# Feed-forward first layers by seven block products in place of eight, and phases that alternate

## Chip, cores and metric

The kernel runs on one core of a Trainium2 chip. The metric is the device time of one execution in microseconds (us).

## What is computed

Attention with a mask by clusters, then two feed-forward networks, all in float32. The attention is not touched by the change; what follows it is:

```python
x = attention(q, k, v, centroids)               # 1536 tokens x 512
p = domain_probs / (domain_probs.sum(-1, keepdims=True) + 1e-9)
y = 0
for e in range(4):                              # first network: w1[e] 512x1024, w2[e] 1024x512
    h = maximum(x @ w1[e], 0)
    y += p[:, e:e+1] * (h @ w2[e])
h = y @ w_in                                    # second network: 512x2048
out = maximum(0.01 * h, h) @ w_out              # 2048x512
```

## The kernel before, in words

The hidden columns of both networks are cut into 24 chunks of 256 (`FCH`): 16 of the first network (`c < N1`, four per expert) and 8 of the second. A chunk has a first layer, h, for three blocks of 512 tokens (`u`), and a second, y, for 12 output tiles of 128 x 512 that add up in `acc`. Float32 accuracy comes from splitting each operand in a high and a low part (hi, lo, of type float32r) and adding three matmuls, hi·hi, hi·lo and lo·hi. So the first layer of a chunk is 3 token blocks x 2 column blocks of 128 x 4 blocks of the 512 model dimensions x 3 = 72 matmuls (`h_products`, L622), and the second is 12 tiles x 2 x 3 = 72 (`emit_y1`, L772 to L774; in the second network `emit_y2`, L790 to L792). All of these have 512 columns.

Behind a block of h (`h_finish`): VectorE forms g from the PSUM result (L634; in the second network ScalarE scales first, L638, and VectorE takes the maximum, L639), ScalarE writes its high part (L119) and GpSimd its low part (L120). Behind a tile of y VectorE adds it to `acc` (L779, L797). The weights of a chunk come by DMA, are split by ScalarE and GpSimd, and in the second network (where the inputs hold 64-bit numbers) are first narrowed by one ScalarE and four VectorE instructions per matrix (L180 to L190).

The order of the work is the order in which the code emits it. The loop at the end runs over the chunks, and the first layer of chunk c+1 is emitted between the tiles of the second layer of chunk c: a block h(c+1, u), then four tiles of y(c), and so on:

```python
for i in range(NTILE):
    if i % KC == 0:
        emit_h(c + 1, i // KC)
    (emit_y1 if c < N1 else emit_y2)(c, i)
```

For this the split weights `w1s`, `w2s` and the split hidden values `hbuf` exist twice, and chunk c uses set c % 2. Set 0 of `w1s` and `hbuf` is made in a pool `early` at the right end of SBUF (it is filled while the attention still runs), set 1 and both sets of `w2s` in the pool `ffn`. In the built program the tiles of `early` start 32 bytes past a multiple of 64 (`w1hi0` at 182240, `hhi0` at 194528), those of `ffn` at multiples of 128. At the step from the first network to the second (chunk 15) the result y is split again as the new x, tile by tile, by ScalarE and GpSimd, and h(16, 0) is emitted ahead of the last four tiles. In PSUM h has two buffers of two banks, y four of one bank.

## Time and profile before

| | us |
|---|---|
| runs | 1059.11, 1059.86, 1064.7; median 1059.86 |
| the profiled execution | 1058.93 |
| its span | 1057.1 |
| TensorE busy in it | 1028.7 (97%), 6182 matmuls |
| VectorE, ScalarE, GpSimd busy | 558.6, 358.9, 457.9 |

The span runs from the first to the last instruction of the profiled execution; its time has 1.83 us around it. Matmuls overlap in the pipeline, so a matmul's own duration (0.39 us) is longer than the distance to the next; distances are read between starts.

### The profile page before, as it was taken

What the parts mean: (1) busy time and instruction counts of PE and PEld (TensorE: products, weight loads), DVE (VectorE), ACT (ScalarE), POOL (GpSimd) and SP (SyncE); (2) the same over time, 40 slices, a digit from 0 to 9 for tenths busy, and PEclk for the clock granted to TensorE, in tenths of its full rate; (3) what the DMA queues carried; (4) which work ended last, traced back from release to release, by engine and by line L of the source; (5) the groups of instructions that cost most, each with busy time, mean ns of one, the idle gap of its engine ahead of it and who ended that gap; (6) DMA issues with size and microseconds to landing.
All of it is one profiled execution on the core that took longest, in us unless ns stands there. A gap on an engine that the chain in (4) does not pass through costs nothing.

```text
span 1057.1 us, 14668 instructions
## 1 busy us (share of the span) xinstructions
PE 1028.7 (97%) x6182; PEld 843.4 (80%) x6184; DVE 558.6 (53%) x744; ACT 358.9 (34%) x435; POOL 457.9 (43%) x232
## 2 busy tenths in 40 slices
PE   7799999999999999999999999999999999999998
PEld 4678888887888888888888888888877888888886
DVE  7698888886113333334333343333572376555754
ACT  3577777784320111101111011110243432323320
POOL 4367777771632433324333343323475333333331
PEclk8899999999999999999999999999999999999999
DMA  7855666440301112111111111110210212212003
GB/s 187 171 119 114 135 136 135 105 104 13 115 15 40 40 40 54 17 40 41 40 46 25 40 40 40 35 46 20 80 42 38 80 51 69 77 43 80 4 37 120
DMA packets 59530, 70.71 MB, mean 67 GB/s; under 512 B 25060, under 2 KB 42088, under 8 KB 59464
## 3 DMA queue, kind: packets, MB, share of 16 engines
q1 hardware_dynamic: 59464, 69.77, 25.2%
q8 instruction: 49, 0.80, 0.3%
q14 instruction: 17, 0.14, 0.0%
HBM read 46.19 MB, written 3.17 MB: 47 GB/s over the span
## 4 chain that ended last, share of the span: by engine, by line
PE 84%; DVE 9%; SPq 2%; POOL 2%; ACT 2%; DMA 1%; issue 1%; DVEq 0%; ACTq 0%
PE big L622 37%; PE y L774 8%; PE y L773 8%; PE y L772 8%; PE y L791 4%; PE y L790 4%; PE y L792 4%; DVE m L401 3%; PE big L397 2%; PE big L432 2%; PE big L433 1%; PE small L458 1%; PE small L460 1%; PE small L459 1%; PE big L266 1%
## 5 line engine op out<-in xcount | busy, mean ns | idle before, releaser
L120 POOL TENSOR_TENSOR hlo<-g,hhi 128x1024 fp32r<-128x1024 f32 x72 | 176.3, 2449 | 446.7 <-ACT hhi L119 446.7
L622 PE MATMUL big<-xlo,w1hi 128*128 128x512 f32 x576 | 226.8, 394 | 1.0 <-POOL xlo L120 1.0
L622 PE MATMUL big<-xhi,w1hi 128*128 128x512 f32 x576 | 226.8, 394 | 0.5 <-DVE xlo L120 0.5
L622 PE MATMUL big<-xhi,w1lo 128*128 128x512 f32 x576 | 226.1, 392 | 0.0
L119 ACT ACTIVATE hhi<-g 128x1024 fp32r<-128x1024 f32 x72 | 76.3, 1060 | 437.2 <-DVE g L634 406.2
L634 DVE SCALAR_TENSOR_TENSOR g<-big,pb 128x1024 f32<-128x1024 f32 x48 | 58.8, 1225 | 241.8 <-PE big L622 234.4
L446 POOL TENSOR_TENSOR plo<-p,phi 128x768 f16<-128x768 f32 x84 | 138.1, 1655 | 82.2 <-ACT phi L445 46.4
L779 DVE TENSOR_TENSOR acc<-y,acc 128x512 f32<-128x512 f32 x180 | 124.1, 691 | 90.5 <-PE y L774 87.7
L774 PE MATMUL y<-hlo,w2hi 128*128 128x512 f32 x384 | 151.2, 394 | 0.0
L772 PE MATMUL y<-hhi,w2hi 128*128 128x512 f32 x384 | 150.7, 392 | 0.5 <-DVE acc L779 0.5
L773 PE MATMUL y<-hhi,w2lo 128*128 128x512 f32 x384 | 150.8, 393 | 0.0
L622 PEld LDWEIGHTS big<-xlo,w1hi 128*128 128x128 f32 x576 | 108.3, 188 | 26.4 <-POOL xlo L120 2.2
L622 PEld LDWEIGHTS big<-xhi,w1hi 128*128 128x128 f32 x576 | 108.2, 188 | 25.6 <-DVE xlo L120 0.9
L622 PEld LDWEIGHTS big<-xhi,w1lo 128*128 128x128 f32 x576 | 108.3, 188 | 24.6
L401 DVE TENSOR_REDUCE m<-big 128x1 f32<-128x768 f32 x96 | 90.3, 949 | 14.1 <-PE big L397 12.9
L435 ACT ACTIVATE p<-big 128x768 f32<-128x768 f32 x96 | 77.6, 809 | 34.7 <-PE big L433 32.8
L772 PEld LDWEIGHTS y<-hhi,w2hi 128*128 128x128 f32 x384 | 72.2, 188 | 17.4 <-DVE acc L779 0.9
L773 PEld LDWEIGHTS y<-hhi,w2lo 128*128 128x128 f32 x384 | 72.1, 188 | 16.6
L774 PEld LDWEIGHTS y<-hlo,w2hi 128*128 128x128 f32 x384 | 72.1, 188 | 16.3
L639 DVE TENSOR_TENSOR g<-big,g 128x1024 f32<-128x1024 f32 x24 | 29.4, 1225 | 88.0 <-ACT g L638 88.0
L791 PE MATMUL y<-w2lo,hhi 128*128 128x512 f32 x192 | 75.5, 393 | 0.0
L790 PE MATMUL y<-w2hi,hhi 128*128 128x512 f32 x192 | 75.4, 393 | 0.0
(134 smaller groups left out, 1577.7 us busy)
## 6 DMA issues: line engine op xcount, KB each, us to landing
qkb<-pair SPq DMA_DIRECT2D x32, 384.0 KB, 6.8
w1raw<-in_moe_w_dram SPq DMA_DIRECT2D x16, 512.0 KB, 3.4
w2raw<-in_moe_w_dram SPq DMA_DIRECT2D x16, 512.0 KB, 3.6
w1raw<-in_moe_w_in_dram SPq DMA_DIRECT2D x8, 1024.0 KB, 5.3
w2raw<-in_moe_w_out_dram SPq DMA_DIRECT2D x8, 1024.0 KB, 4.8
qka<-pair SPq DMA_DIRECT2D x16, 384.0 KB, 4.0
vraw<-in_v_dram SPq DMA_DIRECT2D x16, 192.0 KB, 2.9
pb<-pe_rows SPq DMA_DIRECT2D x4, 768.0 KB, 8.1
```

The lines of the kernel that those rows point to most:

```text
L119: nc.scalar.activation(out=hi, in_=src, func=AF.Copy)
L120: lo_engine.tensor_tensor(out=lo, in0=src, in1=hi.bitcast(F32), op=ALU.subtract)
L401: nc.vector.tensor_reduce(out=m_t[t][:, j:j + 1], in_=ps[:, 0:S], op=ALU.max, axis=AX.X)
L435: nc.scalar.activation(out=p_t[t, kb], in_=ps[:, 0:S], func=AF.Exp, scale=scale)
L446: (nc.vector if plo_on_vector else nc.gpsimd).tensor_tensor(out=plo, in0=p, in1=phi, op=ALU.subtract)
L622: nc.tensor.matmul(pv[:, f, :], lhsT=w[:, kc, fs], rhs=x[:, kc, us], start=kc + i == 0, stop=kc == KC - 1 and i == 2,)
L772: nc.tensor.matmul(ps, lhsT=whi[:, f, ks], rhs=hi[:, f, us], start=f == 0, stop=False)
L773: nc.tensor.matmul(ps, lhsT=wlo[:, f, ks], rhs=hi[:, f, us], start=False, stop=False)
L774: nc.tensor.matmul(ps, lhsT=whi[:, f, ks], rhs=lo[:, f, us], start=False, stop=f == NF - 1)
L779: nc.vector.tensor_tensor(out=a, in0=ps, in1=a, op=ALU.add)
L790: nc.tensor.matmul(ps, lhsT=hi[:, f, ts], rhs=whi[:, f, :], start=f == 0, stop=False)
L791: nc.tensor.matmul(ps, lhsT=hi[:, f, ts], rhs=wlo[:, f, :], start=False, stop=False)
```

## The change

- In the four chunks 0, 1, 16 and 17 (`PLAIN`) the first layer stays at 72 matmuls. In the other 20 (`emit_seven`) token block 0 stays plain (24 matmuls), and blocks 1 and 2 are one 2 x 2 x 2 block product (two column blocks of 128, two halves of 256 model dimensions, two token blocks) by the Strassen-Winograd scheme: seven products of six matmuls each (`product`) in place of eight, 42 in place of 48.
- The scheme needs sums. Of the weights: s1 to s4, four GpSimd instructions of 128 x 256 per chunk and a split of the result (`weights_sums`). Of x: t1 to t4, once per network, by VectorE, ScalarE and one GpSimd instruction (`input_sums`). Of the products: five additions on VectorE (`plus`) and one copy on ScalarE per chunk, through three SBUF tiles `part`; products that belong to one sum are added up in PSUM.
- Instead of h(c+1) between the tiles of y(c), the whole first layer of a chunk runs, then its whole second layer, then the next chunk. There is one set of `w1s`, `w2s` and `hbuf`, which is set 0; the sums s and t lie in `ffn`. PSUM is eight tiles of one bank: 0 to 5 for h, four in turn (6, 7, 2, 3) for y.
- g, hi and lo of h are made per column block, 128 x 512 in place of 128 x 1024; low parts of weights in two halves. The narrowed weights go straight to the raw tiles. The first `acc` copies (chunks 0 and 16) go from ScalarE to VectorE, and a third of the low parts of the new x from GpSimd to VectorE.

What the order of instructions shows, at the three places that matter. First VectorE, in a chunk of the first network: y, big and z are PSUM tiles, pb the probabilities. Before:

```order
L634 SCALAR_TENSOR_TENSOR g0_3478<-big0_5156,pb1_4216 128x1024
L779 TENSOR_TENSOR acc_4218<-y1_5184,acc_4218 128x512
L779 TENSOR_TENSOR acc_4218<-y2_5192,acc_4218 128x512
L779 TENSOR_TENSOR acc_4218<-y3_5200,acc_4218 128x512
L779 TENSOR_TENSOR acc_4218<-y0_5208,acc_4218 128x512
L634 SCALAR_TENSOR_TENSOR g0_3478<-big1_5216,pb1_4216 128x1024
```

Now, from the second column block of token block 0 to the second tile of y:

```order
L656 SCALAR_TENSOR_TENSOR g1_4208<-z1_6074,pb0_3476 128x512
L895 TENSOR_TENSOR part_4218<-z3_6117,part_4218 128x512
L895 TENSOR_TENSOR part_4218<-z4_6131,part_4218 128x512
L656 SCALAR_TENSOR_TENSOR g0_3475<-z2_6075,pb0_3476 128x512
L895 TENSOR_TENSOR part_4218<-z5_6142,part_4218 128x512
L895 TENSOR_TENSOR z4_6131<-z4_6131,part_4218 128x512
L656 SCALAR_TENSOR_TENSOR g0_3475<-part_4218,pb0_3476 128x512
L656 SCALAR_TENSOR_TENSOR g1_4208<-z4_6131,pb0_3476 128x512
L895 TENSOR_TENSOR z5_6142<-z5_6142,part_4218 128x512
L656 SCALAR_TENSOR_TENSOR g1_4208<-z5_6142,pb0_3476 128x512
L944 TENSOR_TENSOR acc_4210<-z7_6173,acc_4210 128x512
L944 TENSOR_TENSOR acc_4210<-z2_6184,acc_4210 128x512
```

The five additions and four of the six g stand together ahead of the first tile of y. TensorE waits for the second and third of these additions before it adds further products into z4 and z5.

Then GpSimd, in a chunk of the first network. Before:

```order
L120 TENSOR_TENSOR hlo1_4214<-g0_3478,hhi1_4213 128x2x512
L120 TENSOR_TENSOR w1lo0_3474<-w1raw_3475,w1hi0_3473 128x1024
L120 TENSOR_TENSOR w2lo1_4212<-w2raw_4217,w2hi1_4211 128x1024
L120 TENSOR_TENSOR hlo1_4214<-g1_4215,hhi1_4213 128x2x512
```

Now:

```order
L192 TENSOR_TENSOR w1lo0_3471<-w1raw_3472,w1hi0_3470 128x512 x2
L204 TENSOR_TENSOR sums_4213<-w1raw_3472 128x256
L205 TENSOR_TENSOR sums_4213<-sums_4213,w1raw_3472 128x256
L206 TENSOR_TENSOR sums_4213<-w1raw_3472 128x256
L207 TENSOR_TENSOR sums_4213<-w1raw_3472,sums_4213 128x256
L192 TENSOR_TENSOR slo_4215<-sums_4213,shi_4214 128x512 x2
L120 TENSOR_TENSOR hlo0_3474<-g1_4208,hhi0_3473 128x512 x2
L192 TENSOR_TENSOR w2lo0_4206<-w2raw_4207,w2hi0_4205 128x512 x2
L120 TENSOR_TENSOR hlo0_3474<-g0_3475,hhi0_3473 128x512 x2
L120 TENSOR_TENSOR hlo0_3474<-g1_4208,hhi0_3473 128x512 x2
```

Five instructions per chunk have become sixteen smaller ones; the split of the weights for the next chunk and their sums now follow the last low parts of h.

And TensorE at a step from the first layer to the second. Before (chunk c in y, chunk c+1 in h):

```order
L774 MATMUL y0_5148<-hlo0_3477,w2hi0_4209 128x512
L622 MATMUL big0_5156<-xhi_66,w1hi1_4207 128x512
L622 MATMUL big0_5156<-xlo_67,w1hi1_4207 128x512
L622 MATMUL big0_5156<-xhi_66,w1lo1_4208 128x512
...
L772 MATMUL y1_5184<-hhi0_3476,w2hi0_4209 128x512
```

Now (the last product of a chunk, and its own y):

```order
L862 MATMUL z5_6142<-xhi_63,shi_4214 128x512
L862 MATMUL z5_6142<-xlo_64,shi_4214 128x512
L862 MATMUL z5_6142<-xhi_63,slo_4215 128x512
...
L937 MATMUL z7_6173<-hhi0_3473,w2hi0_4205 128x512
```

The y that follows reads the h that was just made, from the same set 0. Over the whole program TensorE has 120 rows less (7644 in place of 7764).

The diff, cut to its core:

```diff
-    psum = ctx.enter_context(tc.tile_pool(name="psum", bufs=1, space=bass.MemoryType.PSUM))
 
     st_main = ExitStack()
     st_prep = ExitStack()
     psum_a = st_main.enter_context(tc.tile_pool(name="psum_a", bufs=1, space=bass.MemoryType.PSUM))
-    bigs = [(psum, "big0"), (psum, "big1"), (psum_a, "big2")]
+    bigs = [(psum_a, "big0"), (psum_a, "big1"), (psum_a, "big2")]
     smalls = [(psum_a, "small0"), (psum_a, "small1")]
-    turns = [0, 0]
+    turns = [0, 0, 0]
...
-    def weights_split(c, part):
-
-        if c >= NCH:
-            return []
-        hi, lo = (w1s, w2s)[part][c % 2]
-        if not (wide and chunks[c][3] is None):
-            return [lambda: split(hi, lo, raw12[part], nc.gpsimd)]
+    def weights_narrow(c, part):
 
         w = raw64[part].rearrange("p k (f t) -> p k f t", t=2)
         low, high = w[:, :, :, 0], w[:, :, :, 1]
-        f = ffn.tile(list(hi.shape), F32, tag="narrow", name="narrow", bufs=2)
+        f = raw12[part]
...
-            lambda: split(hi, lo, f, nc.gpsimd),
+        ]
+
+    def split_halves(hi, lo, src):
+
+        nc.scalar.activation(out=hi, in_=src, func=AF.Copy)
+        n = src.shape[1] // 2
+        for x in (slice(0, n), slice(n, 2 * n)):
+            nc.gpsimd.tensor_tensor(out=lo[:, x], in0=src[:, x], in1=hi.bitcast(F32)[:, x], op=ALU.subtract)
+
+    def weights_split(part):
+        hi, lo = (w1s, w2s)[part][0]
+        split_halves(hi, lo, raw12[part])
+
+    def weights_sums():
+
+        r = raw12[0]
+        a11, a12, a21, a22 = [r[:, 2 * k:2 * k + 2, 128 * f:128 * f + 128] for f in range(2) for k in range(2)]
+        s1, s2, s3, s4 = [sums[:, n] for n in range(4)]
+        return [
+            lambda: nc.gpsimd.tensor_tensor(out=s1, in0=a21, in1=a22, op=ALU.add),
+            lambda: nc.gpsimd.tensor_tensor(out=s2, in0=s1, in1=a11, op=ALU.subtract),
+            lambda: nc.gpsimd.tensor_tensor(out=s3, in0=a11, in1=a21, op=ALU.subtract),
+            lambda: nc.gpsimd.tensor_tensor(out=s4, in0=a12, in1=s2, op=ALU.subtract),
+            lambda: split_halves(shi, slo, sums),
         ]
...
-        whi, wlo = w1s[c % 2]
+        whi, wlo = w1s[0]
...
-    def h_finish(c, u):
-        hi, lo = [x[:, :, u * 512:(u + 1) * 512] for x in hbuf[c % 2]]
-        pv = h_ps.pop((c, u)).rearrange("p (f t) -> p f t", f=NF)
-        g = gbuf[u % len(gbuf)]
+    def h_split(c, u, f, src, between=None):
+
+        nf = src.shape[1]
+        hi, lo = [x[:, f:f + nf, u * 512:(u + 1) * 512] for x in hbuf[0]]
+        if nf == NF:
+            g = gbuf[turns[2] // 2 % 2]
+        else:
+            g = gbuf[turns[2] // 2 % 2][:, turns[2] % 2:turns[2] % 2 + 1, :]
+        turns[2] += nf
         if c < N1:
+            if between:
+                between()
             p = pbuf[chunks[c][3] % 2][:, :, u * 512:(u + 1) * 512]
             nc.vector.scalar_tensor_tensor(
-                out=g, in0=pv, scalar=0.0, in1=p.to_broadcast([128, NF, 512]), op0=ALU.max, op1=ALU.mult,
+                out=g, in0=src, scalar=0.0, in1=p.to_broadcast([128, nf, 512]), op0=ALU.max, op1=ALU.mult,
             )
         else:
-            nc.scalar.activation(out=g, in_=pv, func=AF.Copy, scale=0.01)
-            nc.vector.tensor_tensor(out=g, in0=pv, in1=g, op=ALU.max)
+            nc.scalar.activation(out=g, in_=src, func=AF.Copy, scale=0.01)
+            if between:
+                between()
+            nc.vector.tensor_tensor(out=g, in0=src, in1=g, op=ALU.max)
         split(hi, lo, g, nc.gpsimd)
 
+    def h_finish(c, u):
+        h_split(c, u, 0, h_ps.pop((c, u)).rearrange("p (f t) -> p f t", f=NF))
...
-    bigs.pop()
-    smalls[:] = [(psum_f, f"y{n}") for n in range(4)]
-    w1_set(ffn)
     w2_set(ffn)
-    w2_set(ffn)
-    h_set(ffn)
     raw12.append(ffn.tile([128, FCH // 128, DM], F32, name="w2raw"))
+    gbuf.append(ffn.tile([128, FCH // 128, 512], F32, name="g1"))
+    pbuf.append(ffn.tile([128, 1, NT], F32, name="pb1"))
     acc = ffn.tile([128, NTILE * DM], F32, name="acc")
     acc_t = acc.rearrange("p (k t) -> p k t", k=KC)
     acc_n = acc.rearrange("p (i d) -> p i d", i=NTILE)
-    if wide:
-        raw64 = [
-            ffn.tile([128, KC, 2 * FCH], I32, name="w1raw64"), ffn.tile([128, FCH // 128, 2 * DM], I32, name="w2raw64"),
+    raw64 = [
+        ffn.tile([128, KC, 2 * FCH], I32, name="w1raw64"), ffn.tile([128, FCH // 128, 2 * DM], I32, name="w2raw64"),
+    ]
+
+    sums = ffn.tile([128, 4, 2, 128], F32, name="sums")
+    shi, slo = [ffn.tile([128, 4, 2, 128], F32R, name=f"s{x}") for x in ("hi", "lo")]
+    thi, tlo = [ffn.tile([128, 4, 2, 512], F32R, name=f"t{x}") for x in ("hi", "lo")]
+    part = ffn.tile([128, 3, 1, 512], F32, name="part")
+
+    BANKS = ((0, 1), (2, 3), (4, 5))
+
+    def bank(n):
+        return psum_f.tile([128, 1, 512], F32, tag=f"z{n}", name=f"z{n}")
+
+    def y_bank():
+        turns[1] += 1
+        return bank((6, 7, 2, 3)[turns[1] % 4])[:, 0, :]
...
+    def product(ps, w, x, first):
+
+        for k in range(2):
+            for i, j in ((0, 0), (0, 1), (1, 0)):
+                nc.tensor.matmul(
+                    ps[:, 0, :], lhsT=w[i][:, k, :], rhs=x[j][:, k, :], start=first and k + i + j == 0,
+                    stop=k == 1 and i == 1, skip_group_check=True,
+                )
+
...
+    def emit_seven(c, steps):
+
+        w = w1s[0]
+        a11, a12, a21, a22 = [
+            [x[:, 2 * k:2 * k + 2, 128 * f:128 * f + 128] for x in w] for f in range(2) for k in range(2)
         ]
+        s1, s2, s3, s4 = [[x[:, n] for x in (shi, slo)] for n in range(4)]
+        t1, t2, t3, t4 = [[x[:, n] for x in (thi, tlo)] for n in range(4)]
+        x11, x21, x22 = [
+            [x[:, 2 * k:2 * k + 2, 512 * u:512 * u + 512] for x in (xhi, xlo)] for k, u in ((0, 1), (1, 1), (1, 2))
+        ]
+        copy, u2, u3 = part[:, 0], part[:, 1], part[:, 2]
+
+        def some(n):
+            for _ in range(n):
+                if steps:
+                    steps.pop(0)()
+
+        def plus(out, ps, other):
+            nc.vector.tensor_tensor(out=out, in0=ps, in1=other, op=ALU.add)
+
+        p0, p1, pa = bank(0), bank(1), bank(2)
+        after = [] if c + 1 < NCH and is_wide(c + 1) else steps[:]
+        steps = [] if after else steps
+        some(3)
+        plain(c, 0, 0, p0)
+        product(pa, a11, x11, True)
+        h_split(c, 0, 0, p0, lambda: nc.scalar.activation(out=copy, in_=pa, func=AF.Copy))
+        some(2)
+        plain(c, 0, 1, p1)
+        h_split(c, 0, 1, p1)
+        weights_split(1)
+        steps += after
+        some(len(steps))
+        pb = bank(3)
+        product(pb, s2, t2, True)
+        plus(u2, pb, copy)
+        product(pa, a12, x21, False)
+        pc = bank(4)
+        product(pc, s3, t3, True)
+        plus(u3, pc, u2)
+        h_split(c, 1, 0, pa)
+        pd = bank(5)
+        product(pd, s1, t1, True)
+        plus(u3, pd, u3)
+        product(pc, a22, t4, False)
+        plus(pc, pc, u2)
+        h_split(c, 2, 1, u3)
+        h_split(c, 1, 1, pc)
+        product(pd, s4, x22, False)
+        plus(pd, pd, u2)
+        h_split(c, 2, 0, pd)
...
-        ps = small()
+        ps = y_bank()
...
-            nc.scalar.activation(out=a, in_=ps, func=AF.Copy)
+            nc.vector.tensor_copy(out=a, in_=ps)
...
-            split(xhi[:, k, us], xlo[:, k, us], a, nc.gpsimd)
+            split(xhi[:, k, us], xlo[:, k, us], a, nc.gpsimd if u < 2 else nc.vector)
...
-    for u in range(1, NU):
-        emit_h(0, u)
+    turns[1] = 0
+    PLAIN = (0, 1, N1, N1 + 1)
+    sums_left, quota = [], []
     for c in range(NCH):
-        turn = c == N1 - 1
-        steps = weights_split(c + 2, 0) + [lambda: weights_load(c + 3, 0)]
-        steps += weights_split(c + 1, 1) + [lambda: weights_load(c + 2, 1)]
+
+        steps = []
+        if c + 1 < NCH and is_wide(c + 1):
+            steps += weights_narrow(c + 1, 0)
+            if c + 2 < NCH:
+                steps.append(lambda: weights_load(c + 2, 0))
+        if c + 1 < NCH and not is_wide(c + 1):
+            steps.append(lambda: weights_load(c + 1, 1))
+        if c in PLAIN:
+            weights_split(1)
+            if c == 0:
+                sums_left = input_sums(False)
+                quota = [5, 5, 5, 5]
+            n = quota.pop(0)
+            slots = steps + sums_left[:n]
+            sums_left = sums_left[n:]
+            blocks = [(u, f) for u in range(1 if c == 0 else 0, NU) for f in range(NF)]
+            for n, (u, f) in enumerate(blocks):
+                if c > 0:
+                    ps = bank(BANKS[u][f])
+                    plain(c, u, f, ps)
+                elif f == 0:
+                    both_ps = [bank(BANKS[u][f]) for f in range(NF)]
+                    for k in range(KC):
+                        for g in range(NF):
+                            plain(c, u, g, both_ps[g], [k])
+                if c == 0:
+                    ps = both_ps[f]
+                h_split(c, u, f, ps)
+                for _ in range(-(-len(slots) // (len(blocks) - n))):
+                    step = slots.pop(0)
+                    if step:
+                        step()
+        else:
+            emit_seven(c, steps)
...
+            steps.append(lambda: weights_split(0))
+            if c + 1 not in PLAIN:
+                steps += weights_sums()
...
-        steps.reverse()
+        steps = [x for pair in zip_longest(steps, later) for x in pair if x]
         for i in range(NTILE):
-            if i % KC == 0:
-                u = i // KC
-                if turn and u == NU - 1:
-                    emit_h(c + 1, 0)
-                elif not turn and c + 1 < NCH:
-                    emit_h(c + 1, u)
+            if c == N1 - 1 and i == NTILE - 1:
+                sums_left = input_sums(True)
+                quota = [3, 2, 4, 4]
+                sums_left.pop(0)()
             (emit_y1 if c < N1 else emit_y2)(c, i)
-            for _ in range(2 if len(steps) > NTILE - 1 - i else 1):
-                if steps:
-                    steps.pop()()
-        if turn:
-            for u in range(1, NU):
-                emit_h(c + 1, u)
+            for _ in range(-(-len(steps) // (NTILE - i))):
+                steps.pop(0)()
 
 
 # ---- launch: one core; inputs and outputs as the reference has them ----
```

## Rows read from the trace of the kernel before

**Rows 1.** The page, part 1, the whole span.

```profile
span 1057.1 us, 14668 instructions
PE 1028.7 (97%) x6182; PEld 843.4 (80%) x6184; DVE 558.6 (53%) x744; ACT 358.9 (34%) x435; POOL 457.9 (43%) x232
```

**Rows 2.** TensorE, who waited for whom, 250 us to end: us, times, longest.

```profile
PE big L622 <- POOL xlo L120: 1.0, 2, 0.8
PE big L622 <- DVE xlo L120: 0.5, 1, 0.5
PE y L772 <- DVE acc L779: 0.5, 1, 0.5
```

**Rows 3.** Order of time, TensorE: start, us, line, operation; first matmul of a block.

```profile
258.84 0.50 PE L622 MATMUL big<-xhi,w1hi 128*128 128x512 f32 x1 [0.49 <-DVE xlo L120]
...
469.61 0.39 PE L622 MATMUL big<-xhi,w1hi 128*128 128x512 f32 x1
...
475.05 0.40 PE L772 MATMUL y<-hhi,w2hi 128*128 128x512 f32 x1
...
480.66 0.40 PE L622 MATMUL big<-xhi,w1hi 128*128 128x512 f32 x1
...
486.14 0.40 PE L772 MATMUL y<-hhi,w2hi 128*128 128x512 f32 x1
...
502.84 0.39 PE L622 MATMUL big<-xhi,w1hi 128*128 128x512 f32 x1
...
508.45 0.40 PE L772 MATMUL y<-hhi,w2hi 128*128 128x512 f32 x1
...
513.91 0.39 PE L622 MATMUL big<-xhi,w1hi 128*128 128x512 f32 x1
...
536.07 0.39 PE L622 MATMUL big<-xhi,w1hi 128*128 128x512 f32 x1
...
1053.09 0.39 PE L792 MATMUL y<-w2hi,hlo 128*128 128x512 f32 x1
```

**Rows 4.** Order of time: VectorE, ScalarE and GpSimd behind a matmul.

```profile
403.14 0.39 PE L622 MATMUL big<-xhi,w1hi 128*128 128x512 f32 x1
403.34 0.69 DVE L779 TENSOR_TENSOR acc<-y,acc 128x512 f32<-128x512 f32 x1 [0.67 <-PE y L774]
...
475.32 1.23 DVE L634 SCALAR_TENSOR_TENSOR g<-big,pb 128x1024 f32<-128x1024 f32 x1 [4.82 <-PE big L622]
476.57 1.06 ACT L119 ACTIVATE hhi<-g 128x1024 fp32r<-128x1024 f32 x1 [9.84 <-DVE g L634]
477.71 2.41 POOL L120 TENSOR_TENSOR hlo<-g,hhi 128x1024 fp32r<-128x1024 f32 x1 [8.51 <-ACT hhi L119]
```

**Rows 5.** By line, VectorE, 250 us to end: busy us, mean ns, idle before.

```profile
L779 DVE TENSOR_TENSOR acc<-y,acc 128x512 f32<-128x512 f32 x180 | 124.1, 691 | 90.5 <-PE y L774 87.7
L634 DVE SCALAR_TENSOR_TENSOR g<-big,pb 128x1024 f32<-128x1024 f32 x48 | 58.8, 1225 | 241.8 <-PE big L622 234.4 <-POOL hlo L120 7.3
L181 DVE TENSOR_SCALAR narrow<-narrow 128x1024 f32<-128x1024 f32 x16 | 28.5, 1780 | 21.5 <-ACT narrow L180 21.5
L184 DVE TENSOR_SCALAR narrow<-narrow 128x1024 int32<-128x1024 int32 x16 | 11.4, 711 | 0.1
L190 DVE SCALAR_TENSOR_TENSOR narrow<-w2raw,narrow 128x1024 int32<-128x1024 int32 x8 | 11.3, 1417 | 0.0
```

**Rows 6.** By line, ScalarE and GpSimd, 250 us to the end.

```profile
L119 ACT ACTIVATE hhi<-g 128x1024 fp32r<-128x1024 f32 x72 | 76.3, 1060 | 437.2 <-DVE g L634 406.2 <-DVE g L639 31.0
L119 ACT ACTIVATE xhi<-acc 128x512 fp32r<-128x512 f32 x12 | 7.3, 624 | 11.6 <-DVE acc L779 11.6
...
L120 POOL TENSOR_TENSOR hlo<-g,hhi 128x1024 fp32r<-128x1024 f32 x72 | 176.3, 2449 | 446.7 <-ACT hhi L119 446.7
```

**Rows 7.** Order of time, GpSimd, first to second network.

```profile
771.74 1.30 POOL L120 TENSOR_TENSOR xlo<-acc,xhi 128x512 fp32r<-128x512 f32 x1 [3.57 <-ACT xhi L119]
774.92 2.27 POOL L120 TENSOR_TENSOR xlo<-acc,xhi 128x512 fp32r<-128x512 f32 x1 [1.89 <-ACT xhi L119]
```

More of the change, by code (lines that the diff above doesn't have):

```diff
@@ new lines, in product, with plain @@
+    def product(ps, w, x, first):
[5 more added lines that the diff above has]
+                )
+    def plain(c, u, f, ps, ks=range(KC)):
+        us, fs = slice(u * 512, (u + 1) * 512), slice(f * 128, (f + 1) * 128)
+        whi, wlo = w1s[0]
+        for k in ks:
+            for i, (w, x) in enumerate(((whi, xhi), (whi, xlo), (wlo, xhi))):
+                nc.tensor.matmul(
+                    ps[:, 0, :], lhsT=w[:, k, fs], rhs=x[:, k, us], start=k + i == 0, stop=k == KC - 1 and i == 2,
+                )
```

96 lines of the change are left out of this document (77 added, 19 removed).

## Prediction

> **What bounds the kernel now.** I read the page first, for the engine that is full: TensorE, busy 1028.7 of 1057.1 us [rows 1]. Then the list of waits: from the first block of h that belongs to the feed-forward part alone to the end, TensorE waits 2.0 us in all, for low parts of x and one addition into acc [rows 2]. So this part costs the number of matmuls times their distance, and I read distances in order of time [rows 3]. The part begins at 258.84; its last matmul starts at 1053.09 and takes one distance more, 0.23: 794.5 us for 48 matmuls of h(0), 72 of y(0) and 23 x 144 others, 3432.
>
> The reader is to see that there are two distances. From 469.61 to 475.05 stand 24 matmuls of h in 5.44 us, 0.2267 each; from 475.05 to 480.66 24 of y in 5.61, 0.2337. The next h takes 5.48. A chunk later it is the other way round: 24 of h from 502.84 in 5.61, 24 of y in 5.46. From 469.61 to 536.07, two chunks and 288 matmuls, pass 66.46 us, 0.2308 each. The long distance belongs to matmuls that read w1s or hbuf of set 0, in h as stationary operand, in y as moving operand; the short one to those that read set 1. Both sets see the same work on the other engines in turn, so I tie the distance to the set. The sets lie at different places (set 0 in `early`, 32 bytes past a multiple of 64, set 1 at multiples of 128). Why that should matter, no row shows. A short-distance block behind a long-distance one loses 0.02 to 0.04 us at its start (5.46 and 5.48 against 5.44): the long distance lasts about six matmuls into it.
>
> **The change, part by part.** *Fewer matmuls.* 20 chunks x 6 = 120 fewer, 3312 remain. At the mean distance that is 120 x 0.2308 = 27.7 us off.
>
> *One set of buffers, and it is set 0.* This takes part of it back. All y reads hbuf 0, at the long distance; so do, from w1s 0, the plain matmuls of the first layer and the products of a11, a12 and a22. Only the four products of s1 to s4 read neither w1s nor hbuf; sums s and t lie in `ffn` at multiples of 128, so these 24 matmuls per chunk may have the short distance, at best. The long one for certain: 120 in chunk 0, 3 x 144 in chunks 1, 16 and 17, 20 x (72 + 42) in the others, 2832. The short one at best: 20 x 24 = 480. Bounds: 2832 x 0.2337 + 480 x 0.2267 = 770.7 us, and 3312 x 0.2337 = 774.0 if none has it. In the order of products the 24 stand as runs of 6, 12 and 6 among the others. A run of 6 is about as long as the loss at its start, so it gains nothing; a run of 12 gains 12 x 0.007 - 0.04 = 0.05. 20 x 0.05 = 1.0: I take 773.0.
>
> *VectorE, ScalarE, GpSimd.* What they get more of costs nothing as long as TensorE does not wait for it. I checked this by walking a chunk of the first network with the durations of the rows. Prices for 128 x 512: an addition 0.69 [rows 5]; g 0.69 (between 0.61, half of 1.23, and that; I take the addition's, since a fixed part doesn't halve); high part 0.62 [rows 6]; low part 1.30 undisturbed [rows 7] and up to 2.27 beside VectorE. An addition that writes PSUM is not in the trace: between 0.69 and twice that, taken at 0.69 as the nearest row; at twice, the low part of (1, 1) below is 0.7 later. GpSimd at 128 x 256: between 0.65, half of 1.30, and 1.30; the line through 2.41 and 1.30 gives 0.75, which I take. VectorE starts 0.20 after the next matmul's start [rows 4], ScalarE and GpSimd 0.1 or less behind their forerunner.
>
> Six matmuls are 1.40 us. Counted from the chunk's start, the products of the first layer end at 4.2 (a11), 8.4 (s2), 9.8 (a12), 11.2 (s3), 12.6 (s1), 14.0 (a22), 15.4 (s4). VectorE: the second addition, which frees z4 for a22, runs from 11.4 to 12.1, and a22 wants to begin at 12.6. Then g(1, 0) to 12.8, the third addition to 13.5; s4, which needs it, wants to begin at 14.0. Half a microsecond of room each. Then the addition on z4 to 14.9, g(2, 1) 15.6, g(1, 1) 16.3, the last addition 17.0, g(2, 0) 17.7. ScalarE and GpSimd behind it: low part of (1, 1) at 18.8, of (2, 0) at 20.1. The second layer begins at 15.4 with token block 0, ready long before; its token block 1 begins 24 matmuls later, at 21.0, block 2 at 26.6. Room 2.2 us. The twelve additions into acc then follow TensorE tile by tile. GpSimd goes on with the next w1 to 22.7, the sums to 25.7, their low parts to 29.4, and the next chunk (from 32.2) needs these only 8 us in. GpSimd's sixteen instructions are 12 x 1.30 + 4 x 0.75 = 18.6 of 32.2 us. The weights have more than a first layer's time between load and use, as before.
>
> *The second network* is tighter. Per chunk VectorE has eight narrowing instructions, at most 2 x 1.78 + 2 x 0.71 + 4 x 1.42 = 10.7 [rows 5], six g and five additions at 0.69, and twelve additions into acc: 26.6 us of 32.2. ScalarE scales ahead of each g, which makes the chain longer: by the same walk the low part of (1, 1) is there at 19.5 against 21.0, and the first addition into acc ends at 20.2, where the fifth tile of y, in the same bank, wants to begin at 21.0. Room 0.8 us, the least I find.
>
> *From attention to the first chunk* TensorE's order is the same up to h(0, 1), whose wait at 258.84 stays. *At the step between the networks* 1.5 of the 2.0 us of waits lie; h(16, 0) no longer stands ahead of the last tiles, so the x it needs is far behind it. VectorE has twelve additions, four low parts, four narrowing instructions and one sum there, some 19 us against 16.8 of y(15). Bounds: all 1.5 saved, or 2 us more lost; I keep 1.0 as lost.
>
> *Sum.* 773.0 + 1.0 = 774.0 against 794.5: 20.5 us less. From the profiled execution's 1058.93 that is 1038.4. The median of the runs shown is 0.9 higher; from its 1059.86 it is **1039.4 us**.
>
> **Rivals.** *The distance does not go by set.* The Trainium skill, "Advanced Engine Details and Errata", SBUF Cachelines, says that SBUF has lines of 16 bytes and that accesses that hit the same line run at full performance. By that rule both sets, which start at multiples of 32 bytes, would read alike, and the sum would be the one at the mean distance. In numbers: 3312 x 0.2308 = 764.4 us, 30.1 less than 794.5, 1029.8 us. Against it stands every pair of blocks [rows 3]; for it, that no row tells which property of set 0 does it. Chance 0.05.
>
> *The alternation opens a gap at each phase change.* The chain of additions, g, high and low part has one set of h to write into, and the second layer stands right behind it. If it is late by 2.9 us more than in my walk (2.2 us of room), TensorE waits 0.7 us per chunk, 14 us: 1053. In the second network 1.5 us suffice, for six chunks. For it: the room of 0.8 us there, and ScalarE's place in the chain. Against it: durations that I took from rows with the same neighbours [rows 4]. [...] Chance 0.12.
>
> *GpSimd becomes the bound: slower.* One low part of 128 x 512 took 2.27 us beside VectorE [rows 7], not 1.30. Were all sixteen instructions of a chunk like it, small ones too, GpSimd would need 36.3 us per chunk. Before, a chunk takes 33.2 (66.46 / 2), so 20 x 3.1 = 62 us more: 1122 us. It decides from 2.08 us per instruction (33.2 / 16). For it: VectorE now works on SBUF alone more often. Against it: 72 low parts at a mean of 2.45 for 1024 columns [rows 6], while VectorE added. The Trainium skill, "SBUF — State Buffer", SBUF: two separate sides, says that a port pair shared by VectorE and GpSimd is locked for a whole instruction when VectorE reads two operands from SBUF. Per chunk of the first network VectorE has one instruction with two operands in SBUF. Chance 0.03.
>
> That the matmuls are not fewer is excluded: TensorE's order has 120 rows less.
>
> **How the numbers follow.** The forecast has 0.80, and its own range is 1036 (770.7 and nothing lost at the step) to 1043 (774.0, 2 us more lost there, and 1 to 2 us of small waits in the second network). The range to hold 8 in 10 adds the smaller half of the gap rival and 3 us below for a distance that is only partly tied to set 0: 1033 to 1047. It leaves out the first rival, the last one and the larger gaps. A measurement of this kernel can tell 0.5% from no change, 5.3 us. Faster by more than that, below 1054.6: the forecast, the first rival and 0.09 of the gaps, 0.94. Within it: the largest gaps, 0.03. Slower: GpSimd, 0.03.
>
> **What would show it.** Blocks of 24 matmuls at 5.61 us in every y and plain h, products of s in between them at nearly the same distance; TensorE's waits still around 2 us from 250 us on; chunks of 32.2 us. Wrong is the forecast if y takes 5.44 (the set was not it), if TensorE waits for low parts of h or for acc by tens of us, or if GpSimd's idle time is gone.

## The result, and the profile after

The changed kernel takes 1046.26 us (median of four runs, 1044.78 to 1047.64), the kernel before 1061.15 in runs on the same chip: ratio 0.9863, 95% interval 0.9847 to 0.988. Forecast were 1039.4 us and a gain of 20.5; the gain is 14.9. The sign and the range (1033 to 1047) hold, the narrower range that the prediction gave for the forecast itself (1036 to 1043) doesn't. So 5.6 us have to be found.

The profiled execution took 1047.64 us. Its page, part 1, against [rows 1]:

```profile
span 1045.9 us, 15196 instructions
PE 1012.0 (97%) x6064; PEld 824.5 (79%) x6064; DVE 674.9 (65%) x964; ACT 400.9 (38%) x554; POOL 602.2 (58%) x468
```

VectorE, ScalarE and GpSimd have 303 us more to do in all, and TensorE is still the full one. Who TensorE waited for from 250 us on (us, times, longest), against [rows 2]:

```profile
PE z L955 <- DVE acc L960: 2.2, 1, 2.2
PE z L872 <- DVE g L656: 1.7, 1, 1.7
PE z L937 <- DVE acc L944: 0.4, 1, 0.4
```

The low parts of x are gone from the list, and the sum is 4.3 us instead of 2.0. The first row is in y(16) and the third in y(15), at the step between the networks; the second is the start of the feed-forward part. None is a phase change of a chunk by seven products. Block starts on TensorE in order of time (start, us, line, operation), against [rows 3]; the last two rows are a chunk of the second network:

```profile
391.12 0.39 PE L872 MATMUL z<-xhi,w1hi 128*128 128x512 f32 x1
...
406.43 0.40 PE L937 MATMUL z<-hhi,w2hi 128*128 128x512 f32 x1
...
423.24 0.39 PE L872 MATMUL z<-xhi,w1hi 128*128 128x512 f32 x1
...
880.90 0.40 PE L872 MATMUL z<-xhi,w1hi 128*128 128x512 f32 x1
...
896.19 0.39 PE L955 MATMUL z<-w2hi,hhi 128*128 128x512 f32 x1
```

The seven products and the plain block take 15.31 us for 66 matmuls, y 16.81 for 72 (0.2335 each), the chunk 32.12. The other chunks by seven products ahead of chunk 15 repeat this to 0.01 us. In the second network y takes 16.86. The ends that the prediction walked to, in the same two chunks (VectorE, ScalarE, GpSimd in order of time):

```profile
409.86 1.30 POOL L120 TENSOR_TENSOR hlo<-g,hhi 128x512 fp32r<-128x512 f32 x1
...
898.93 1.31 POOL L120 TENSOR_TENSOR hlo<-g,hhi 128x512 fp32r<-128x512 f32 x1 [0.58 <-ACT hhi L119]
900.13 2.57 DVE L962 TENSOR_TENSOR acc<-z,acc 128x512 f32<-128x512 f32 x4
```

GpSimd begins the first chunk's last low part, (2, 0), at 409.86, back to back with that of (1, 1), which is so done 18.7 us into the chunk (forecast 18.8). In the second network (1, 1) is done at 900.24, 19.3 us in (19.5). The first of four additions into acc ends 0.68 us after 900.13, 19.9 in (20.2).

**Where it was lost: the step between the networks.** y(15) takes 17.49 us instead of 16.81, y(16) 20.88 instead of 16.86. VectorE by line from 759.75 to 815 us (busy us, mean ns, idle before it and who ended it):

```profile
L944 DVE TENSOR_TENSOR acc<-z,acc 128x512 f32<-128x512 f32 x12 | 8.0, 680 | 1.0 <-PE z L939 1.0
L960 DVE COPY acc<-z 128x512 f32<-128x512 f32 x11 | 7.2, 684 | 1.9 <-POOL pb L810 1.1 <-PE z L957 0.7
L120 DVE TENSOR_TENSOR xlo<-acc,xhi 128x512 fp32r<-128x512 f32 x4 | 4.7, 1187 | 2.8 <-ACT xhi L119 2.8
```

The four low parts take 4.7 us and wait 2.8 more for ScalarE's high parts, 7.5 together. The rest of the queue waits with them. In order of time, on all engines:

```profile
777.24 0.39 PE L872 MATMUL z<-xhi,w1hi 128*128 128x512 f32 x1
...
785.26 0.69 DVE L120 TENSOR_TENSOR xlo<-acc,xhi 128x512 fp32r<-128x512 f32 x1 [0.70 <-ACT xhi L119]
...
799.38 0.69 DVE L663 TENSOR_TENSOR g<-z,g 128x512 f32<-128x512 f32 x1 [1.19 <-ACT g L660]
799.99 1.38 DVE L810 TENSOR_TENSOR sums<-acc,pb 128x1024 f32<-128x1024 f32 x1
...
801.30 1.27 DVE L960 COPY acc<-z 128x512 f32<-128x512 f32 x2
...
802.12 0.47 PE L955 MATMUL z<-w2hi,hhi 128*128 128x512 f32 x1 [2.24 <-DVE acc L960]
```

TensorE leaves y(15) at 777.24; VectorE is done with its last low part 8.7 us later. All six g of h(16) stand behind that, a sum of the new x behind them, and the copy that frees the first y bank begins at 801.30, though its tile was done at about 795.5. TensorE waits 2.24 us. Then matmuls stand 0.43 us apart for a while. The stretches by time (window and length; busy time of PE, PEld, VectorE, ScalarE, GpSimd; granted clock, DMA share, GB/s) show the granted clock at 0.61 there, so mostly at the lower of its two levels (1.2 and 2.4 GHz). An earlier stretch looks alike:

```profile
243.30:248.00 4.70, 4.62 (x39) 4.04 (x40) 3.75 (x7) 2.47 (x4) 0.00 (x0) 0.64 0.02 3
802.10:806.40 4.30, 4.28 (x12) 3.42 (x13) 3.22 (x5) 2.53 (x3) 4.30 (x4) 0.61 0.00 0
```

**And at the start.** Counted from the last qka pair behind which TensorE waited for m (231.02 us after, 228.09 before), h(0, 1) begins 34.09 us later instead of 30.75. GpSimd, SP's queue and TensorE in the order of time, before and then after:

```profile
228.09 0.62 PE L397 MATMUL big<-qka 96*128 96x512 f32 x2 [0.81 <-DVE m L401]
232.76 3.01 POOL L120 TENSOR_TENSOR w1lo<-w1raw,w1hi 128x1024 fp32r<-128x1024 f32 x1 [0.65 <-ACT w1hi L119]
235.80 0.37 SPq L165 DMA_DIRECT2D w1raw<-in_moe_w_dram  x1
236.22 0.76 SPq L419 DMA_DIRECT2D qka<-mrow  x1
239.49 0.47 PE L432 MATMUL big<-qka 128*128 128x512 f32 x1 [1.16 <-ACT p L435]
```

```profile
231.02 0.62 PE L412 MATMUL big<-qka 96*128 96x512 f32 x2 [0.83 <-DVE m L416]
235.69 3.87 POOL L192 TENSOR_TENSOR w1lo<-w1raw,w1hi 128x512 fp32r<-128x512 f32 x2 [0.65 <-ACT w1hi L189]
239.59 0.37 SPq L163 DMA_DIRECT2D w1raw<-in_moe_w_dram  x1
240.00 0.75 SPq L434 DMA_DIRECT2D qka<-mrow  x1
243.38 0.76 PE L447 MATMUL big<-qka 128*128 128x512 f32 x1 [2.11 <-DMA qka<-mrow]
...
263.75 1.22 DVE L656 SCALAR_TENSOR_TENSOR g<-big,pb 128x1024 f32<-128x1024 f32 x1
...
265.11 0.47 PE L872 MATMUL z<-xhi,w1hi 128*128 128x512 f32 x1 [1.72 <-DVE g L656]
```

The first w1's low part is now two instructions of 512 columns, 3.87 us instead of 3.01. SP's load of the next w1 overwrites what they read and waits; the small copy of mrow stands behind it on SP's queue and is issued 0.85 us later in the chain (8.98 after the pair instead of 8.13). TensorE waits 2.11 us, and the clock falls. At 265.11 it waits for g(0, 0), which nothing in h(0, 1) reads: its banks come from a pool that opens when the attention's pool has been read for the last time.

**The account of the profiled pair.** The spans differ by 11.2 us, 9.3 less than 20.5. Of that, 2.9 (231.02 - 228.09) were lost ahead of the mark: near 42 us TensorE's wait for a load of q was 5.0 against 2.0 us. In the runs below the mark lies anywhere from 228.8 to 231.7, at 230.1 also in run 3, which has the order of the kernel before; whether the change has a part in it, no run shows. The start took 3.3, the step 3.7 (0.68 + 4.02, of which 1.0 was forecast), the end behind the last matmul 0.5; all other matmuls came 1.2 cheaper than forecast (1041.63 - 265.11 = 776.5, less 4.7, is 771.8 against 773.0). The sum is 9.2 of the 9.3. The 0.5 at the end is the same in all profiles: 4.3 us behind the last matmul with the changed order, 3.8 with the order before; why, no run shows.

### The profile page after: what moved, and what is told of

Its sections match the earlier page's. It is cut to its first block, busy times and chain, and to the rows that moved or that the text cites. A ratio compares the mean times of both kernels' runs of the same rounds, so it can differ in the third digit from the quotient of the medians.

```text
span 1045.9 us, 15196 instructions
## 1 busy us (share of the span) xinstructions
PE 1012.0 (97%) x6064; PEld 824.5 (79%) x6064; DVE 674.9 (65%) x964; ACT 400.9 (38%) x554; POOL 602.2 (58%) x468
## 4 chain that ended last, share of the span: by engine, by line
PE 70%; DVE 3%; ACT 1%; issue 0%; POOL 0%; DVEq 0%; POOLq 0%
PE z L862 18%; PE z L872 15%; PE z L939 8%; PE z L938 8%; PE z L937 8%; PE z L955 4%; PE z L957 4%; PE z L956 4%; ACT xhi L119 0%; DVE xlo L120 0%; DVE acc L944 0%; DVE g L663 0%; POOL hlo L120 0%; DVE w2raw L173 0%; DVE w2raw L182 0%
## 5 line engine op out<-in xcount | busy, mean ns | idle before, releaser
L120 POOL TENSOR_TENSOR hlo<-g,hhi 128x512 fp32r<-128x512 f32 (+1 forms) x143 | 198.5, 1396 | 293.7 <-ACT hhi L119 292.3
L944 DVE TENSOR_TENSOR acc<-z,acc 128x512 f32<-128x512 f32 x180 | 124.0, 690 | 101.5 <-PE z L939 101.4
L119 ACT ACTIVATE hhi<-g 128x512 fp32r<-128x512 f32 (+1 forms) x143 | 89.5, 635 | 189.7 <-DVE g L656 143.9
L939 PE MATMUL z<-hlo,w2hi 128*128 128x512 f32 x384 | 152.9, 398 | 0.0
L938 PE MATMUL z<-hhi,w2lo 128*128 128x512 f32 x384 | 151.6, 395 | 0.0
L937 PE MATMUL z<-hhi,w2hi 128*128 128x512 f32 x384 | 150.9, 393 | 0.4 <-DVE acc L944 0.4
L872 PE MATMUL z<-xhi,w1hi 128*128 128x512 f32 x248 | 98.2, 396 | 1.7 <-DVE g L656 1.7
L872 PE MATMUL z<-xlo,w1hi 128*128 128x512 f32 x248 | 98.4, 397 | 0.0
L872 PE MATMUL z<-xhi,w1lo 128*128 128x512 f32 x248 | 98.2, 396 | 0.0
L939 PEld LDWEIGHTS z<-hlo,w2hi 128*128 128x128 f32 x384 | 72.1, 188 | 16.8
L956 PE MATMUL z<-w2lo,hhi 128*128 128x512 f32 x192 | 76.8, 400 | 0.0
```

The lines of the kernel that those rows point to most:

```text
L120: lo_engine.tensor_tensor(out=lo, in0=src, in1=hi.bitcast(F32), op=ALU.subtract)
L872: nc.tensor.matmul(ps[:, 0, :], lhsT=w[:, k, fs], rhs=x[:, k, us], start=k + i == 0, stop=k == KC - 1 and i == 2,)
L937: nc.tensor.matmul(ps, lhsT=whi[:, f, ks], rhs=hi[:, f, us], start=f == 0, stop=False)
L938: nc.tensor.matmul(ps, lhsT=wlo[:, f, ks], rhs=hi[:, f, us], start=False, stop=False)
L939: nc.tensor.matmul(ps, lhsT=whi[:, f, ks], rhs=lo[:, f, us], start=False, stop=f == NF - 1)
L944: nc.vector.tensor_tensor(out=a, in0=ps, in1=a, op=ALU.add)
```

## The experiments

Theory: the matmuls cost what set 0's place makes them cost, the walk through a chunk is right, and what is missing was lost at the two ends of the attention and of the first network. All runs: median of four, beside the kernel before at 1060.8 to 1061.1 in the same runs.

**1 to 3. Where set 0 lies.** One unused tile at the end of `early`, of 24 or 8 elements (96 or 32 bytes). Set 0 starts 96 bytes past a multiple of 128 (182240 is 1423 x 128 + 96), and the pool ends at a fixed place, so the tile moves set 0 down: by 96 bytes to a multiple of 128 (run 1, and run 3 in the kernel before), by 32 to 64 past one (run 2).

```diff
         h_set(early)
+        early.tile([128, 24], F32, name="pad")
         weights_load(0, 0)
```

> The changed kernel with 96 unused bytes behind the last tile of the pool `early`, so that set 0 (w1s, hbuf) begins at a multiple of 128 instead of 32 bytes past a multiple of 64; nothing else moves. Theory (the start address of set 0 makes the long distance): every y block of 72 takes 72 x 0.2267 = 16.3 us instead of 16.8, a seven chunk 138 x 0.2267 = 31.3 instead of 32.1, and the time falls by about 2832 x 0.007 = 20 us, from 1046 to about 1026; no other engine has to get faster for that, but the room before the additions into acc shrinks with it, so up to 3 us may come back as waits. Rival (something else of set 0 makes it: its pool, its end of the memory, or that it is the set on which all the work runs): 1046, y still 16.8.

> The same with 32 bytes: set 0 begins at a multiple of 64 that is not one of 128. Theory with 64 as the step that counts: as with 96 bytes, about 1026. Theory with 128 as the step: unchanged, 1046, y 16.8. A value between would say that the distance grows with the offset. Rival (not the address): unchanged, as with 96 bytes.

> The kernel before with the same 96 bytes, both sets then at multiples of 128. Theory (address): the blocks of set 0 come down to 5.44 us per 24 as well, 1716 x 0.007 = 12.0 us, and the loss of 0.02 to 0.04 us at each of some 46 changes between the sets goes too, about 1 us: 1061 - 13 = 1048. Rival (something else of set 0): 1061.

Measured: 1027.22 us with 96 bytes (ratio to before 0.9682, 0.9661 to 0.9703), 1041.78 with 32 (1038.62 to 1044.11), and 1047.05 for the kernel before with 96, 1.0 below the 1048 expected. Block starts on TensorE, y, h and y, with 96 bytes, then two pairs with 32 bytes (y in the first network, y in the second):

```profile
338.96 0.39 PE L938 MATMUL z<-hhi,w2hi 128*128 128x512 f32 x1
...
355.28 0.39 PE L873 MATMUL z<-xhi,w1hi 128*128 128x512 f32 x1
...
370.24 0.39 PE L938 MATMUL z<-hhi,w2hi 128*128 128x512 f32 x1
```

```profile
340.22 0.40 PE L938 MATMUL z<-hhi,w2hi 128*128 128x512 f32 x1
...
356.72 0.39 PE L873 MATMUL z<-xhi,w1hi 128*128 128x512 f32 x1
...
856.33 0.39 PE L956 MATMUL z<-w2hi,hhi 128*128 128x512 f32 x1
...
873.13 0.40 PE L873 MATMUL z<-xhi,w1hi 128*128 128x512 f32 x1
```

With 96 bytes y takes 16.32 (0.2267 each) and the chunk 31.28: the start address makes the distance, and an idle pad is worth 19.0 us here and 14.0 in the kernel before. At a multiple of 64 that is not one of 128, y takes 16.50 where hbuf is the moving operand (first network) and 16.80 where it is the stationary one (second network): 64 is not enough, and the time between the two forecasts comes from these two cases. One block of that run, y(0), took 16.79 with hbuf moving; why, no run shows. The waits at the step stay: y(15) and y(16) took 17.45 and 21.20 in the run with 96 bytes.

**4. One operand's place.** w1s 32 bytes past a multiple of 128, hbuf at a multiple (three pads in `early`).

> The changed kernel with w1s at 32 bytes past a multiple of 128 and hbuf at a multiple of 128, by three unused pads in `early`. Theory A (a matmul has the long distance if one of its own operands begins off a multiple of 128): plain first layers stay at 16.86 per 72 and y comes down to 16.32 in both networks; the seven chunk 42 x 0.2337 + 24 x 0.2267 + 16.3 = 31.6; time 1046 - 24 x 0.5 = 1034. Rival B (only hbuf's place counts): 1027, as with both at 128. Rival C (one set off the multiple slows all): 1046.

Measured: 1033.63 us. Starts of a plain h, the y behind it, and a later y, h, y:

```profile
288.95 0.39 PE L875 MATMUL z<-xhi,w1hi 128*128 128x512 f32 x1
...
305.75 0.40 PE L940 MATMUL z<-hhi,w2hi 128*128 128x512 f32 x1
...
337.43 0.40 PE L940 MATMUL z<-hhi,w2hi 128*128 128x512 f32 x1
...
353.77 0.39 PE L875 MATMUL z<-xhi,w1hi 128*128 128x512 f32 x1
...
369.07 0.40 PE L940 MATMUL z<-hhi,w2hi 128*128 128x512 f32 x1
```

Plain h 16.80, y 16.34, the chunk 31.64: theory A to 0.06 us, and the time to 0.4. Each matmul pays for its own operands.

**5. The change taken apart.** All chunks plain, phases alternating, one set (`PLAIN = range(NCH)`, no sums of x or w1).

> The changed kernel with no chunk by seven products: all 24 first layers are 72 plain matmuls, the phases alternate, one set of buffers as in the changed kernel; the sums of x are left out with it. This takes the change apart. Theory (alternation by itself costs nothing at the phase changes; the one set costs the long distance on every matmul): 3432 x 0.2337 = 802.1 against 794.5, +7.6, the start +1.2, the step between the networks +0 to +4: 1070 to 1074, some 25 to 28 us above the changed kernel, TensorE's waits from 270 us on under 5 us. Rival (alternation opens a gap at each of 48 phase changes, and the seven products happen to fill it): waits of 14 us or more, 1084 or above.

Measured: 1073.25 us; waits from 255 us on are the 1.7 for g(0, 0) alone. So the seven products gain 27.0 us, and what they are bought with, alternation and the one set, costs 12.4. Between the profiles it is 12.3: 8.2 from h(0, 1) to the last matmul (802.7 against 794.5, the long distance on every matmul), 1.8 at the start, 0.5 at the end and 1.8 ahead of the mark. No phase change opens a gap. The step between the networks is clean too (y(15) 16.79, y(16) 16.86): without the additions of the seven-product chunk ahead of it and the sums of the new x, VectorE is in time there. So the loss at the step belongs to the seven products and their sums: on the matmuls alone they gain 30.9 us (802.7 - 771.8), and 4.7 of that are lost again at the step.

**6. How much room a chunk has.** Four more additions in the chain, in the code behind the fourth of the five, not the third:

```diff
         plus(pc, pc, u2)
+        for _ in range(4):
+            plus(copy, pc, u2)
```

> The changed kernel with four needless additions of 128x512 on VectorE in each seven chunk, behind the third addition (the result goes to an unused part), some 2.5 us more in the chain ahead of g(2, 1), g(1, 1) and the last addition. Theory (the walk of the prediction, whose ends the changed kernel's trace shows: low part of (1, 1) at 18.8 us of the chunk in network 1 against 21.0, first addition into acc at 19.9 in network 2 against 20.9): network 1 loses 0 to 0.5 us per chunk, network 2 some 1.5 to 1.9 us in each of 6 chunks, 9 to 12 us in all: 1055 to 1060, all waits there named acc. Rival A (the room is larger than walked, other work gives way): 1046. Rival B (no room at all, every microsecond of the chain shows): 20 x 2.5 = 50 us more, 1096.

Measured: 1064.82 us, 18.6 more, none of the three sums. By place: 0.25 us in each of 13 chunks of the first network (3.3), 2.13 in each of six of the second (12.8), 1.3 at the step. The four delay the chain by 2.9 us, not 2.5 (in the chunk below g(2, 1) begins 3.52 us behind the start of the fourth addition; 0.61 without them). Less the walk's room of 0.8 us that is 2.1 per chunk of the second network, as measured; in the first, less 2.2, it would be 0.7, so the room there is larger than walked. The mechanism is the walk's; the total took the delay too small and left out the first network and the step. The wait, with what VectorE did:

```profile
873.10 2.48 DVE L964 TENSOR_TENSOR acc<-z,acc 128x512 f32<-128x512 f32 x4
...
873.93 0.48 PE L957 MATMUL z<-w2hi,hhi 128*128 128x512 f32 x1 [1.90 <-ACT hhi L119]
```

This matmul reads hi parts that were there long before; what it needs is the bank that the first addition, done at about 873.7, frees. The row names ScalarE because that came last by the profile.

**7 and 8. The step between the networks.** First the copies into acc on ScalarE (`nc.scalar.activation(out=a, in_=ps, func=AF.Copy)` for chunks 0 and 16), then instead of that the low parts:

```diff
-            split(xhi[:, k, us], xlo[:, k, us], a, nc.gpsimd if u < 2 else nc.vector)
+            split(xhi[:, k, us], xlo[:, k, us], a, nc.gpsimd)
```

> The changed kernel with the first copies into acc (chunks 0 and 16) on ScalarE again, as they were before the change. Theory (VectorE is some 7 us late behind y(15), because its low parts of x wait for ScalarE's high parts and g(16) stands behind them; both engines are late together): ScalarE's copies stand behind its last scale and high part of h(16), which wait for VectorE, so y(16) keeps 18.5 to 20.9 us and the time stays within 2.5 us of 1046. Rival (the twelve copies themselves are what VectorE has no time for): y(16) falls to 16.9 and the time by 4 us, to 1042.

> The changed kernel with all twelve low parts of the new x (end of y(15)) on GpSimd; the changed kernel gives the last four to VectorE. Theory (VectorE is 7 us behind TensorE at the end of y(15) because each of these four stands in its queue behind a ScalarE high part and waits 0.70 us for it, 4 x (0.70 + 0.69) = 5.6 us with the low parts; g(16) and the first copies into acc stand behind them): y(15) 16.8 instead of 17.5 us, y(16) 16.9 to 18 instead of 20.9, the granted clock stays at 1.00 in y(16), and the time falls by 3.5 to 4.7 us to about 1042. Rival (the narrowing instructions, the sums of the new x and the copies are too much by themselves): y(16) stays above 19.5 us, the time within 1.5 us of 1046.

Measured: 1044.49 us and 1042.41. With the copies moved, y(16) is 18.91, as the theory had it, and TensorE waits 1.4 us for ScalarE's copy instead. With the low parts moved, y(16) is 17.06, and no wait is left in it (starts of y(16) and of the next h):

```profile
793.35 0.40 PE L955 MATMUL z<-w2hi,hhi 128*128 128x512 f32 x1
...
810.41 0.39 PE L872 MATMUL z<-xhi,w1hi 128*128 128x512 f32 x1
```

So y(16) was late by the queue behind VectorE's low parts, not by the copies. In other profiles y(16) took 19.35 with a wait of 2.25 us and the granted clock at 1.00; against these the low parts are worth 2.3 us. They don't do it alone: run 5 has the same four on VectorE, each with its wait of 0.70 us, and the last is done 6.7 us behind y(15), but VectorE catches up. In the changed kernel it has three sums of the new x to do ahead of the first copy besides (4.3 us); the loss takes both. y(15) stays at 17.48, against the expected 16.8, so the low parts don't hold it. The trace shows four narrowing instructions of the next w2 between VectorE's additions there; the first takes 1.83 us in the changed kernel and 0.70 in run 5, where y(15) is 16.79. No run tests this.

**9 to 11. The start.** One pair of banks in a pool of its own, first with z0 and z1 as halves of one tile, then with the pool closed behind h(0, 1); and apart from that the first w1's low part in one piece:

```diff
-        weights_split(0)
+        hi, lo = w1s[0]
+        split(hi, lo, raw12[0], nc.gpsimd)
```

> The changed kernel with one pair of PSUM banks (big1, later z0 and z1) in a pool of its own that stays open over the whole kernel, as two pairs were before the change; h(0, 1) goes there, and nothing else moves. Theory (h(0, 1) waits 1.72 us for g(0, 0) because its banks come from a pool that opens only when all readers of the attention's pool are done; in the kernel before it waits 0.49 us for the low part of x): the wait for g goes, one of about 0.5 us for xlo takes its place, h(0, 1) begins 30.7 to 31.2 us after the last qka pair that TensorE waited for near 231 instead of 32.4, and the time falls by 1.2 to 1.7 us, which the times alone can't settle. Rival (h(0, 1) starts late because ScalarE and VectorE deliver xhi and xlo late): same distance, 32.4, with the wait put down to xlo.

> The attempt on the banks mended: h(0, 1) again goes to a pair of banks of a pool that is open through the attention, but the pool closes behind h(0, 1), and z0 and z1 come from a new one as two tiles. In the first attempt both halves were one tile, and the plain chunks waited for g of the first half before the second could be written. Theory (h(0, 1) waits for g(0, 0) by the opening of the new pool alone): h(0, 1) begins right behind h(0, 0), 30.4 to 30.6 us after the last qka pair that TensorE waited for near 231, or 32.1 where the granted clock falls behind the wait for mrow, against 32.4 and 34.1 without the edit; no wait of more than 0.5 us from there to y(15); the time falls by 1.9 us. Rival (the first attempt gained nothing at the start, 32.06 against 32.4, since something else sets it): 32.1 also where the clock stays at 1.00.

> The changed kernel with the low part of the first w1 (the one in the attention) as one GpSimd instruction of 1024 columns again; the changed kernel does it in two of 512, 3.87 us instead of 3.01. Theory (SP's load of the next w1 waits for it, and the copy of mrow into qka stands behind that load on SP's queue): the load is issued 7.7 us after the last qka pair that TensorE waited for near 231 instead of 8.56, TensorE waits 1.0 to 1.2 us instead of 2.0 near 242, the granted clock stays at 1.00 in the 4.7 us behind it, h(0, 1) begins 31.5 us after that pair instead of 32.4, and the time falls by 0.9 us and by up to 1.6 more against an execution whose clock fell there. Rival (the wait near 242 has to do with the banks or with the loads of q and k at the start): 32.4.

Measured: 1055.63, 1044.71 and 1043.57 us. The first was a miss of my own making: a plain matmul into one half of the tile now waits for g of the other. Its row; then the pair and h(0, 1) in the second; then the pair and SP's and TensorE's rows in the third:

```profile
786.62 0.79 PE L879 MATMUL big<-xhi,w1hi 128*128 128x512 f32 x1 [7.22 <-DVE g L664]
```

```profile
230.64 0.61 PE L414 MATMUL big<-qka 96*128 96x512 f32 x2 [0.84 <-DVE m L418]
...
262.87 0.40 PE L879 MATMUL big<-xhi,w1hi 128*128 128x512 f32 x1
```

```profile
229.29 0.61 PE L412 MATMUL big<-qka 96*128 96x512 f32 x2 [0.84 <-DVE m L416]
...
237.00 0.37 SPq L163 DMA_DIRECT2D w1raw<-in_moe_w_dram  x1
...
240.72 0.47 PE L447 MATMUL big<-qka 128*128 128x512 f32 x1 [1.17 <-ACT p L450]
...
261.25 0.47 PE L873 MATMUL z<-xhi,w1hi 128*128 128x512 f32 x1 [1.72 <-DVE g L656]
```

With the banks mended, h(0, 1) begins 32.23 us after the pair in an execution whose clock fell to 0.64 behind mrow, where the changed kernel has 34.09: the wait for g(0, 0) costs 1.9 us, of which y(0) takes 0.55 back (17.36). With the low part in one piece the load is issued 7.71 after the pair, the wait is 1.17, the clock stays at 1.00, and h(0, 1) begins at 31.96; without the edit it is 32.40 to 32.56 in executions whose clock stayed, so the later mrow costs 0.44 to 0.60 by itself (expected 0.9) and some 1.6 more where the clock falls. By their times alone runs 7, 10 and 11 can't be told from the changed kernel: their ratios' intervals, 0.9823 to 0.9862 in all, overlap with 0.9847 to 0.988. What they show is in the traces. Run 8's interval, 0.9813 to 0.9842, lies below.

**12. All four together.**

> All four together: set 0 at a multiple of 128, all low parts of the new x on GpSimd, the first w1's low part in one piece, h(0, 1) in banks of its own. Theory (the costs lie at different places and add): 1046.3 - 19.0 (address, as measured) - 6.0 (the step between the networks as it stands in the run with the address alone: 17.45 + 21.2 against 2 x 16.32) - 1.1 (mrow) - 1.9 (banks) = 1018, range 1016 to 1021; TensorE's waits from 255 us on under 1 us. Rival (with the shorter matmuls VectorE becomes what the step between the networks waits for, or the next transfer in the attention is as late as mrow): 1023 or more, with waits of over 1.5 us there.

Measured: 1022.96 us (1021.37 to 1023.6), ratio to before 0.9638, 0.9623 to 0.9653: 23 us less than the changed kernel. Theory's 1018 is missed; the four don't add. h(0, 1) begins 29.99 us after the pair, but TensorE then waits 1.3 us for acc in y(0):

```profile
PE z L946 <- DVE acc L951: 1.3, 2, 0.9
```

So y(0) takes 18.20 instead of 16.32: VectorE's sums of x stand ahead of the first copies there, and h(0) is now too early for them. At the step y(15) and y(16) take 17.41 and 17.33, 2.1 above 2 x 16.32. The rival has its time (1023), and by half its cause: the next wait is VectorE's in both places, but at the step none is over 0.6 us.

## Why the prediction was right, and where it was not

- *Fewer matmuls, at set 0's distance.* Right. At the long distance all plain chunks would take 802.1 us and the changed ones 773.0, 29.1 less; found are 802.7 (run 5) and 771.8, 30.9 less, and y runs at 0.2335. In the time the gain is 27.0, since the step takes part of it back. Of the 1.2 below 773.0, some is that the runs of six matmuls with s gained a little too (1.36 to 1.39 us, not 1.40).
- *The distance goes by the place of the set.* Right, and now by cause: the rival at 1029.8 fell with y at 16.81. The Trainium skill, "Advanced Engine Details and Errata", SBUF Cachelines, from which that rival worked out that both sets would read alike, doesn't give the measured distances: by lines of 16 bytes 32, 64 and 96 bytes of offset would all do no harm, and they cost up to 0.5 us per 72 matmuls.
- *The walk through a chunk.* Right to 0.3 us at each of three ends. The rival of the gap at each phase change fell: no wait there, and run 6 shows where it would begin: 2.9 us more in the chain cost 2.1 per chunk of the second network and 0.25 in the first.
- *GpSimd as the bound.* It is busy 602.2 of 1045.9 us, and a chunk's end never waits for it. Fell.
- *"At the step between the networks" (1.0 lost).* Mis-sized: 3.2 us where the clock stays, 4.7 in the profile. The sum took VectorE's four low parts at their durations; they cost 7.5 us instead of 2.8, since each stands in order behind a high part of another engine, and two took 1.7 us beside GpSimd's. Run 8 gives 3.9 us back by that one edit. The balance also stopped at the end of y(15): run 5, with the same low parts but without the sums of the new x that come behind them, loses nothing. The 0.7 us in y(15) isn't in that; its cause stays untested.
- *"From attention to the first chunk TensorE's order is the same up to h(0, 1), whose wait at 258.84 stays."* Wrong. TensorE's order is the same, but not what it waits for: GpSimd's low part is cut in two, and SP's queue carries the delay to mrow (0.44 to 0.60 us, 2.1 where the clock fell); and the banks of h(0, 1) come from a pool that opens later (1.3 us at least: 31.96 against 30.65 in the kernel before with 96 bytes). Runs 10 and 11 show both. The prediction priced the low parts in halves in every chunk and overlooked the one ahead of them.
- *The clock.* Not in the prediction. It cost 1.5 us at the step and 1.6 at the start of the profiled execution.
- *The range.* That 1046.26 lies inside 1033 to 1047 is in part luck. Its upper end was put there for small waits in the second network and for the smaller half of the gap rival. Neither came; the start and the clock, which the prediction had at nothing, used up that margin.

Against the paired median, 5.6 us are to be explained: 2.2 to 3.7 at the step and 1.8 to 3.4 at the start, by whether the clock falls, and 0.5 at the end, less 1.2 on the matmuls, are 3.3 to 6.4. How often the clock falls in unprofiled executions stays open; at the rates of the profiles below it is 4.6 (an estimate), and the ratio's interval alone is 1.7 us to either side.
